# Choosing 80 tokens per expert by counting ranks, with the column copies beside the expert matmuls, in an HGRN scan followed by a capacity-limited expert layer

## The chip, the cores and the metric

One core of a Trainium2 chip runs the whole program. The metric is the time of one execution on the device in microseconds (us), as a median over runs. Times inside the program come from one execution taken by the profiler.

## The reference, cut to what matters

```python
# x, f_logit: (4, 5056, 256); lower_bound: (256,); w_gate: (256, 8)
# w1: (8, 256, 1024); w2: (8, 1024, 256); capacity = 80; all float32
f = lb + (1 - lb) * sigmoid(f_logit)
for t in range(S):                       # S = 5056, per batch and channel
    h = f[:, t] * h + (1 - f[:, t]) * x[:, t];  y[:, t] = h
x = y.reshape(20224, 256)
logits = x @ w_gate;  expert = argmax(logits);  gate = softmax(logits)[expert]
out = zeros((20224, 256))
for e in range(8):
    tok = tokens of expert e, the 80 with the largest gate
    out[tok] = gate[tok] * (relu(x[tok] @ w1[e]) @ w2[e])
```

Every token is scanned, but only 640 of the 20,224 output rows are other than zero.

## The kernel before

The scan works with channels on the 128 partitions. A unit is 512 tokens of one batch: 4 batches times 10 groups give 40 units. `load` fetches the two inputs on SP's queue, `gate` takes the sigmoid on ACT, `enter` multiplies on POOL, `to_channels` transposes both into PSUM on PE (tile tags `sp` and `up`, a bank each, two buffers for `sp` and four for `up`), `decay` writes the decay factors into `h_all` on ACT, and `scan` runs the recurrence in `h_all` on DVE, half of the channels at a time. `logits` (PE) gives the router's logits one unit later, and once for each group of four units `by_token` (an ACT copy `ls` and PE transposes `lt`) and `choice` (four DVE operations) give each token's expert and its distance to the other logits. `h_all` holds all tokens, 158 KB of each partition, and stays until the copies are done.

The kernel is under a manual schedule: each engine carries out its instructions in the order in which the program text emits them. The software pipeline is the loop over `n` at the end of the scan part, in which iteration `n` emits the load of unit `n+3`, `gate` and `enter` of `n+2`, the transposes and `decay` of `n+1`, `scan` of `n`, `logits` of `n-1`, and `by_token` and `choice` when unit `n-2` ends a group. In two places of the loop (after group 4 and after group 9) `gates` finishes five groups in one go: an exponential on ACT, sums and reciprocals on DVE, and for each group two DVE products, a PE transpose and a DVE copy into `cand`.

`cand` has 128 rows, which are 8 experts times 16 (4 batches, and the token's number modulo 4), with 1,264 gate values each; a token's value is in the row of its expert, and the other seven have zero.

Then come, one after the other: `largest(cand)`, which takes the 80 largest of each row with ten rounds of three DVE operations over the row; a trip through DRAM that lays the 16 lists of an expert side by side in `cand2` (8 rows of 1,280); `largest(cand2)`, another ten rounds; eight indirect DMAs that fetch the token numbers; and the copies of 640 columns of `h_all` into `xe`, by DVE, ACT and POOL, each of which first loads 16 token numbers into its registers. Only then is `h_all`'s room given to the weights of experts 1 to 7 (14 of 16 MB), and the experts run: `hidden(e)` scales the columns (DVE), multiplies by `w1` (PE, 32 matmuls) and applies relu (ACT), `result(e)` multiplies by `w2` (PE, 16 matmuls), scales by the gate (DVE) and scatters 80 rows into `out` (POOL). `hidden(e+1)` is emitted before `result(e)`. The zeros of `out` are written by 40 DMAs on SP's queue while the lists are made.

Of the kernel before, what the change touches and what calls it, by code (L numbers as in the profile page):

```python
# [16 lines left out]
P = 128  # L17
TOP = 8
# [4 lines left out]
def kernel(  # L23
# [23 lines left out]
    K = (capacity + TOP - 1) // TOP * TOP  # L47
    assert N % P == 0 and D % P == 0 and F % P == 0 and S % R == 0 and C * E == P
# [14 lines left out]
    def tiles(ap, b, g):  # L63
# [25 lines left out]
    base_row = consts.tile([1, P], F32, name="base_row")  # L89
    nc.gpsimd.iota(base_row, pattern=[[0, E], [S, B], [1, R]], base=0, channel_multiplier=0,  # L90
                   allow_small_or_imprecise_dtypes=True)
    base = consts.tile([P, 1], F32, name="base")
    list_base = consts.tile([E, 1], F32, name="list_base")
    nc.gpsimd.iota(list_base, pattern=[[0, 1]], base=0, channel_multiplier=C * K,
                   allow_small_or_imprecise_dtypes=True)

    cand = consts.tile([P, SEG], F32, name="cand")
    BATCHES = 2
    per_batch = -(-n_grp // BATCHES)
    shift = consts.tile([P, per_batch, C, E], F32, name="shift")  # L100
    nc.gpsimd.memset(shift, 0.0)
    pick = consts.tile([P, n_grp, C], F32, name="pick")

# [4 lines left out]

    with tc.tile_pool(name="ld", bufs=4) as ld, \
# [5 lines left out]
        xs, fs, sts, uts, sps, ups, lgs, lts, gms = ({} for _ in range(9))  # L115
# [6 lines left out]
        def setup():  # L122
            nc.vector.tensor_scalar(omlb, lb, -1.0, 1.0, ALU.mult, ALU.add)
            nc.vector.tensor_scalar(nomlb, lb, 1.0, -1.0, ALU.mult, ALU.add)
            for o in range(DC):
                nc.vector.tensor_scalar_mul(wg[:, o], wg[:, o], omlb[:, ds(o, 1)])
            bp = plg.tile([P, 1], F32, name="bp", tag="lt")
            nc.tensor.transpose(bp, base_row, ident[:1, :1])
            nc.vector.tensor_copy(base, bp)

# [56 lines left out]


        def choice(g):
# [3 lines left out]

            def small(shape, name):
                return gsm.tile([P] + shape, F32, name=name, tag=name)[:n_p]

            mx = small([C], "mx")
            nc.vector.tensor_reduce(mx, lg, AX.X, ALU.max)
            sh = shift[:n_p, g - begin(g)]
            nc.vector.tensor_tensor(sh, lg, mx.unsqueeze(2).broadcast_to(full), ALU.subtract)  # L200
            eq = small([C, E], "eq")
# [6 lines left out]
        def gates(g0, g1):  # L208
            n = g1 - g0
            sh = shift[:, ds(0, n)]  # L210
            nc.scalar.activation(sh, sh, ACT.Exp)
            sm = gsm.tile([P, n, C], F32, name="sm", tag="sm")
            nc.vector.tensor_reduce(sm, sh, AX.X, ALU.add)
            nc.vector.tensor_scalar_add(sm, sm, 1e-9)
            gt = gsm.tile([P, n, C], F32, name="gt", tag="gt")
            nc.vector.reciprocal(gt, sm)
            for g in range(g0, g1):
                n_p = rows(g)
                gm = gsm.tile([P, E, C], F32, name="gm", tag="gm", bufs=2)[:n_p]
                full = [n_p, C, E]  # L220
                oh = gsm.tile([P, C, E], F32, name="oh", tag="oh")[:n_p]
                nc.vector.tensor_tensor(oh, revexp[:n_p].unsqueeze(1).broadcast_to(full),
                                        pick[:n_p, g].unsqueeze(2).broadcast_to(full),
                                        ALU.is_equal)
                nc.vector.tensor_tensor(
                    gm.rearrange("p e c -> p c e"), oh,
                    gt[:n_p, g - g0].unsqueeze(2).broadcast_to(full), ALU.mult)
                gms[g] = gm
                candidates(g)

        def candidates(g):
            n_p = rows(g)
            ct = plg.tile([P, P], F32, name="ct", tag="lt")
            nc.tensor.transpose(ct[:, :n_p], gms.pop(g).rearrange("p e c -> p (e c)"),
                                ident[:n_p, :n_p])
            nc.vector.tensor_copy(cand[:, ds(first(g) // R, n_p)], ct[:, :n_p])
# [9 lines left out]

        ends = sorted({n_grp * i // BATCHES - 1 for i in range(1, BATCHES + 1)} - {-1})
        batches = {g: (ends[i - 1] + 1 if i else 0, g + 1) for i, g in enumerate(ends)}
        AHEAD = 3

        def begin(g):
            return next(g0 for g0, g1 in batches.values() if g0 <= g < g1)

        setup()
        for n in range(-AHEAD, n_unit + 4):
# [10 lines left out]
            group(lambda g: gates(*batches[g]) if g in batches else None, n - 3)  # L266


    EARLY = 1
    w1_sb, w2_sb = [], []  # L270

    def weights(pool, e):
        w1_sb.append(pool.tile([P, DC, F], F32, name=f"w1_sb{e}"))
        nc.sync.dma_start(out=w1_sb[e], in_=w1[e].rearrange("(o p) f -> p o f", p=P))
        w2_sb.append(pool.tile([P, FC, D], F32, name=f"w2_sb{e}"))
        nc.sync.dma_start(out=w2_sb[e], in_=w2[e].rearrange("(c p) d -> p c d", p=P))

    wpool = ctx.enter_context(tc.tile_pool(name="wpool", bufs=1))
    for e in range(EARLY):
        weights(wpool, e)  # L280

    xpool = ctx.enter_context(tc.tile_pool(name="xpool", bufs=1))
    zpool = ctx.enter_context(tc.tile_pool(name="zpool", bufs=1))
    ZR = 4
    zero = zpool.tile([P, ZR * D], F32, name="zero")
    nc.gpsimd.memset(zero, 0.0)
    out_z = out.rearrange("(p k) d -> p (k d)", p=P)
    for k in range(0, N // P, ZR):
        n = min(ZR, N // P - k) * D
        nc.sync.dma_start(out=out_z[:, ds(k * D, n)], in_=zero[:, :n])  # L290

    with tc.tile_pool(name="sel", bufs=1) as sel, \
         tc.tile_pool(name="psl", bufs=1, space=PSUM) as psl, \
         tc.tile_pool(name="psh", bufs=2, space=PSUM) as psh, \
         tc.tile_pool(name="psy", bufs=2, space=PSUM) as psy:


        def largest(src, vals, at):
            for k in range(0, K, TOP):
                top = vals[:, ds(k, TOP)]  # L300
                nc.vector.max(out=top, in_=src)  # L301
                nc.vector.max_index(out=at[:, ds(k, TOP)], in_max=top, in_values=src)  # L302
                if k + TOP < K:
                    nc.vector.match_replace(out=src, in_to_replace=top, in_values=src,  # L304
                                            imm_value=-2.0)

        val = sel.tile([P, K], F32, name="val")
        at = sel.tile([P, K], U32, name="at")
        largest(cand, val, at)
        nc.scalar.dma_start(out=val_dram, in_=val)  # L310
        atf = sel.tile([P, K], F32, name="atf")
        nc.gpsimd.tensor_copy(atf, at)
        ids = sel.tile([P, K], I32, name="ids")
        nc.gpsimd.tensor_scalar(out=ids, in0=atf, scalar1=float(R), scalar2=base,
                                op0=ALU.mult, op1=ALU.add)
        nc.scalar.dma_start(out=id_dram, in_=ids)

        cand2 = sel.tile([E, C * K], F32, name="cand2")
        nc.scalar.dma_start(out=cand2, in_=val_dram.rearrange("(e c) k -> e (c k)", e=E))
        val2 = sel.tile([E, K], F32, name="val2")  # L320
        at2 = sel.tile([E, K], U32, name="at2")
        largest(cand2, val2, at2)
        if capacity < K:
            nc.vector.memset(val2[:, capacity:], -1.0)
        at2f = sel.tile([E, K], F32, name="at2f")
        nc.vector.tensor_copy(at2f, at2)
        nc.vector.tensor_scalar_add(at2f, at2f, list_base)  # L327


        sp = psl.tile([K, 2, E], F32, name="slots")  # L330
        nc.tensor.transpose(sp[:, 0], at2f, ident[:E, :E])  # L331
        nc.tensor.transpose(sp[:, 1], val2, ident[:E, :E])
        place = sel.tile([K, E], I32, name="place")
        nc.vector.tensor_copy(place, sp[:, 0])
        gsl = sel.tile([K, E], F32, name="gsl")
        nc.vector.tensor_copy(gsl, sp[:, 1])
        far = sel.tile([K, E], F32, name="far")
# [3 lines left out]
        id_list = id_dram.rearrange("r k -> (r k)").unsqueeze(1)  # L341
        tok = sel.tile([K, E], I32, name="tok")
        for e in range(E):
            nc.gpsimd.indirect_dma_start(
                out=tok[:, ds(e, 1)], out_offset=None, in_=id_list,
                in_offset=bass.IndirectOffsetOnAxis(ap=place[:, ds(e, 1)], axis=0))
        tokf = sel.tile([K, E], F32, name="tokf")
        nc.vector.tensor_copy(tokf, tok)
        goals = []
        for e in range(E):  # L350
# [96 lines left out]
```

## Time and profile before

| | us |
|---|---|
| median of 3 runs (407.60 to 407.68) | 407.61 |
| the profiled execution | 407.11 |
| its span, first to last instruction | 405.3 |
| DVE busy | 255.1 (63%) |
| PE busy (PE weight loads 153.0) | 200.4 (49%) |
| ACT busy | 134.2 (33%) |
| POOL busy | 129.5 (32%) |

The span is what the timeline's clock counts from; 1.8 us of the profiled execution lie around it. Engines are PE (matmul), PEld (its weight loads), DVE (vector), ACT (scalar), POOL (GpSimd) and SP (which only issues DMAs here); a q behind an engine is its instruction queue. No engine is busy for much more than half of the time, so the busy shares don't say what bounds the kernel: one has to go through its stages in order of time.

### The profile page before, as it was taken

To read this page: it belongs to the slowest core of one execution; us is meant where nothing else is said; L and a number is where in the kernel's file an instruction comes from. 1 tells how busy PE (TensorE), PEld (TensorE's weight loads), DVE (VectorE), ACT (ScalarE), POOL (GpSimd) and SP (SyncE) were. 2 spreads that over 40 slices of the span, in tenths; PEclk is the share of its full clock that TensorE was granted. 3 is DMA by queue.
4 is the path that set the end of the run, shared out by engine and by line. 5 is a ranking of instruction groups with operands and counts; after the bars stand their busy time and mean duration, and the time that the engine had idled before them with its cause. 6 is when DMAs were issued, how large, how long until landed. Compare 5 with 4: busy or idle time off the path is not lost. (4 is left out here: it accounts for less than half of the span.)

```text
span 405.3 us, 5826 instructions
## 1 busy us (share of the span) xinstructions
PE 200.4 (49%) x1718; PEld 153.0 (38%) x1718; DVE 255.1 (63%) x553; ACT 134.2 (33%) x408; POOL 129.5 (32%) x197
## 2 busy tenths in 40 slices
PE   2988999972999996200000000000000039998995
PEld 2866676751766763000000000000000039776773
DVE  0768889886788886699994999942556640001000
ACT  4776767670667763000000000001666501100010
POOL 4868677742477660000000000035670000001001
PEclk9999999996899998555555555555555555999999
DMA  8999999990699926999953000000000029997000
GB/s 245 348 350 349 327 330 281 334 327 20 195 322 320 318 94 204 421 420 420 420 235 134 8 0 1 0 0 0 2 2 1 2 81 377 374 380 266 18 8 16
DMA packets 60015, 80.59 MB, mean 199 GB/s; under 512 B 3400, under 2 KB 52680, under 8 KB 59984
## 3 DMA queue, kind: packets, MB, share of 16 engines
q1 hardware_dynamic: 58496, 79.44, 56.6%
q0 software_dynamic: 640, 0.66, 0.6%
q8 instruction: 13, 0.21, 0.2%
q10 hardware_dynamic: 848, 0.13, 0.2%
q14 instruction: 18, 0.15, 0.1%
HBM read 58.77 MB, written 21.45 MB: 198 GB/s over the span
## 5 line engine op out<-in xcount | busy, mean ns | idle before, releaser
L146 POOL TENSOR_TENSOR x_t<-f_t,x_t 128x1024 f32<-128x1024 f32 x40 | 94.8, 2369 | 53.3 <-ACT f_t L142 41.2
L165 DVE TENSOR_TENSOR_SCAN h_all<-h_all,up 128x512 f32<-128x512 f32 x80 | 95.1, 1253 | 6.9 <-PE up L152 5.7
L375 ACT COPY xe<-h_all 128x2 f32 x256 | 26.2, 190 | 134.2 <-issue 134.2
L159 ACT ACTIVATE h_all<-sp,nomlb 128x512 f32<-128x512 f32 x80 | 50.9, 684 | 44.0 <-PE sp L152 44.0
L394 PE MATMUL h_ps<-xt,w_sb 128*128 128x80 f32 x256 | 36.6, 313 | 55.6 <-DVE xt L386 50.9
L394 PEld LDWEIGHTS h_ps<-xt,w_sb 128*128 128x128 f32 x256 | 35.6, 227 | 58.3 <-DVE xt L386 51.1
L152 PE MATMUL sp<-ident,f_t 128*128 128x128 f32 x320 | 45.9, 290 | 4.2 <-ACT f_t L142 4.2
L152 PE MATMUL up<-ident,x_t 128*128 128x128 f32 x320 | 45.5, 284 | 5.0 <-DVE h_all L165 2.8
L331 PE MATMUL slots<-ident,at2f 8*80 8x8 f32 x1 | 0.2, 200 | 96.4 <-DVE at2f L327 96.4
L177 PE MATMUL lg<-h_all,wg 128*32 128x128 f32 x640 | 44.2, 404 | 6.4 <-ACT ls L182 4.8
L142 ACT ACTIVATE f_t<-f_t 128x1024 f32<-128x1024 f32 x40 | 42.4, 1061 | 9.7 <-DMA f_t<-in_f_logit_dram 9.7
L406 DVE TENSOR_SCALAR y<-y_ps,gsl 80x256 f32<-80x256 f32 x8 | 3.8, 480 | 63.9 <-PE y_ps L403 63.9
L152 PEld LDWEIGHTS sp<-ident,f_t 128*128 128x128 f32 x320 | 37.6, 148 | 16.0 <-ACT f_t L142 10.8
L375 DVE COPY xe<-h_all 128x2 f32 x256 | 30.5, 179 | 19.6 <-issue 19.6
L152 PEld LDWEIGHTS up<-ident,x_t 128*128 128x128 f32 x320 | 38.2, 147 | 7.5 <-DVE h_all L165 3.9
L331 PEld LDWEIGHTS slots<-ident,at2f 8*80 8x80 f32 x1 | 0.1, 135 | 96.7 <-issue 96.7
L407 POOL DMA_INDIRECT out_dram<-y,goal x8 | 7.4, 920 | 90.0 <-DMA w_sb<-in_moe_w_dram 45.6
L301 DVE MAX8 val<-cand 128x8 f32<-128x1264 f32 (+1 forms) x20 | 29.6, 1480 | 5.9 <-DMA cand<-val_dram 5.1
L403 PE MATMUL y_ps<-w_sb,hid 128*80 128x256 f32 x128 | 29.6, 386 | 0.0
L302 DVE FIND_INDEX8 at<-val,cand 128x8 uint32<-128x1264 f32 (+1 forms) x20 | 29.4, 1471 | 0.0
L397 ACT ACTIVATE hid<-h_ps 128x480 f32<-128x480 f32 (+1 forms) x16 | 7.0, 438 | 64.2 <-PE h_ps L394 64.2
L304 DVE MATCH_REPLACE8 cand<-val,cand 128x1264 f32<-128x1264 f32 (+1 forms) x18 | 26.3, 1461 | 0.0
(57 smaller groups left out, 139.8 us busy)
## 6 DMA issues: line engine op xcount, KB each, us to landing
f_t<-in_f_logit_dram SPq DMA_DIRECT2D x40, 512.0 KB, 5.4
x_t<-in_x_dram SPq DMA_DIRECT2D x40, 512.0 KB, 5.7
out_dram<-zero SPq DMA_DIRECT2D x39, 512.0 KB, 10.0
w_sb<-in_moe_w_dram SPq DMA_DIRECT2D x16, 1024.0 KB, 12.8
out_dram<-zero SPq DMA_DIRECT2D x1, 256.0 KB, 2.0
tok<-id_dram,place POOLq DMA_INDIRECT x8, 2.2
out_dram<-y,goal POOLq DMA_INDIRECT x8, 2.3
val_dram<-val ACTq DMA_DIRECT2D x1, 40.0 KB, 1.5
```

The lines of the kernel that those rows point to most:

```text
L142: nc.scalar.activation(sts[n], sts[n], ACT.Sigmoid, scale=-1.0)
L146: nc.gpsimd.tensor_tensor(uts[n], sts[n], uts[n], ALU.mult)
L152: nc.tensor.transpose(ps[:, ds(r * P, P)], src[n][:, r, ds(o * P, P)], ident)
L159: nc.scalar.activation(h_all[:, o, ds(spot(n), G)], sps.pop((n, o)), ACT.Identity, scale=nomlb[:, ds(o, 1)], bias=1.0)
L165: nc.vector.tensor_tensor_scan(h, h, ups.pop((n, o)), h_all[:, o, ds(spot(n) - 1, 1)] if n >= B else 0.0, ALU.mult, ALU.add)
L177: nc.tensor.matmul(lgs[g][ds(r * LC, LC), b], wg[:, o], hv[:, o, :, r], start=o == 0, stop=o == DC - 1, skip_group_check=True)
L301: nc.vector.max(out=top, in_=src)
L302: nc.vector.max_index(out=at[:, ds(k, TOP)], in_max=top, in_values=src)
L304: nc.vector.match_replace(out=src, in_to_replace=top, in_values=src, imm_value=-2.0)
L375: copy(xe[:, :, ds(k + j, 1)], h_all[:, :, ds(v, 1)])
L394: nc.tensor.matmul(h_ps[:, c], w1_sb[e][:, o, ds((c0 + c) * P, P)], xt[:, o], start=o == 0, stop=o == DC - 1, skip_group_check=True)
L403: nc.tensor.matmul(y_ps, hid[:, c], w2_sb[e][:, c], start=c == 0, stop=c == FC - 1)
```

## The change

The branch, the selection, the weights, the copies and the schedule of the gates are new; the scan's own operations are as before. In words:

- The gates are finished in four batches of groups (0 to 3, 4 to 6, 7 and 8, 9), one small job for each loop iteration (`todo`). The product with the reciprocal moves from DVE to POOL. The transposes of a batch share one PSUM bank, `ct`, and `up` has three buffers instead of four.
- `peaks` takes the eight largest of each of 12 parts of every row of `cand` as soon as the part is there (every second column of up to 256). After the loop, the 16 largest of these 96 are the row's candidates.
- A matmul with `mates` gives every row the 256 candidates of its expert, and 16 operations, one for each candidate of a row, count how many are larger. A candidate is taken when the count is under 80. Sums over the rows ahead of it give its slot; 16 matmuls of 80 columns put token numbers and gates into their slots. No list goes through DRAM.
- Four flags for each row say whether 16 candidates might have been too few (`doubts`). They are summed by a matmul beside the experts, and after the experts a branch runs the old lists and the experts again if the sum is over zero.
- Weights come as halves of 512 KB into a ring of seven buffers that has room beside `h_all`: three keys (3 MB) ahead of the selection, the others as the ring's buffers come free.
- Zeros are written by 20 DMAs of 1 MB on ACT's queue, from a source of 2 KB of each partition that is read four times, after the last gates and ahead of the copies.
- Copies of expert `e+2` are emitted ahead of the matmuls of expert `e+1`: 28 columns on DVE, 28 on ACT, 24 on POOL, with one load of as many token numbers each.

```diff
-         tc.tile_pool(name="psu", bufs=4, space=PSUM) as psu, \
+         tc.tile_pool(name="psu", bufs=3, space=PSUM) as psu, \
...
+    def clear(engine, k):
+        n = min(4 * ZW, N // P - k)          # ZW = 2
+        m = n // ZW
+        engine.dma_start(out=out_z[:, ds(k * D, n * D)].rearrange("p (m z) -> p m z", m=m),
+                         in_=zero.unsqueeze(1).broadcast_to([P, m, ZW * D]))
+    clears = range(0, N // P, 4 * ZW)
...
+        def work(g0, g1):
+            jobs = [[lambda: exponentials(g0, g1)], [lambda: sums(g0, g1)]]
+            for g in range(g0, g1 + 1):
+                jobs.append(([lambda g=g: gated(g)] if g < g1 else [])
+                            + ([lambda g=g: turned(g - 1)] if g > g0 else []))
+            jobs.append([lambda: candidates(g0, g1)])
+            mine = [i for i in range(NP) if parts[i][0] == g1 - 1]
+            for i in range(0, len(mine), 2):
+                jobs.append([lambda j=j: peaks(j) for j in mine[i:i + 2]])
+            return jobs
...
+        while n < n_unit + 3 or todo:
...
             group(by_token, n - 2)
             group(choice, n - 2)
-            group(lambda g: gates(*batches[g]) if g in batches else None, n - 3)
+            for job in todo[:1]:
+                for f in job:
+                    f()
+            del todo[:1]
+            group(lambda g: todo.extend(work(*batches[g])) if g in batches else None, n - 2)
+            n += 1
...
+    wring = ctx.enter_context(tc.tile_pool(name="wring", bufs=7))
+    order = [(1, 0)]
+    for e in range(E):
+        order += ([(1, e + 1)] if e + 1 < E else []) + [(2, e)]
...
+    for key in order[:3]:
+        w_sb[key] = weights(*key)            # two DMAs of 512 KB on SP's queue
+    for k in clears:
+        clear(nc.scalar, k)
...
+        nc.vector.max(out=vals[:, :TOP], in_=flat_tops)
+        nc.vector.match_replace(out=rest, in_to_replace=vals[:, :TOP], in_values=flat_tops,
+                                imm_value=-2.0)
+        nc.vector.max(out=vals[:, TOP:], in_=rest)
+        nc.vector.tensor_tensor(spread, ...)                 # 128 x 256
+        nc.tensor.matmul(rivals, mates, spread, ...)
+        for k in range(0, DEEP, TOP):                        # DEEP = 16
+            nc.vector.max_index(out=at[:, ds(k, TOP)], in_max=vals[:, ds(k, TOP)],
+                                in_values=cand)
+        for k in range(DEEP):
+            nc.vector.tensor_scalar(beat, rivals, vals[:, ds(k, 1)], 0.0, ALU.is_gt, ALU.add,
+                                    accum_out=rank[:, ds(k, 1)])
...
+        nc.vector.tensor_scalar(put, at_slot, off[:, 0:1], None, ALU.is_equal)   # 128 x 1280
+        for j in range(DEEP):
+            nc.tensor.matmul(flat_p, what[:, DEEP - 1 - j].rearrange("p i e -> p (i e)"),
+                             put[:, j], start=j == 0, stop=j == DEEP - 1)
+        nc.vector.tensor_copy(trow, flat_p[:E])
...
+    ways = [(mybir.EngineType.DVE, nc.vector.tensor_copy, 28),
+            (mybir.EngineType.Activation, nc.scalar.copy, 28),
+            (mybir.EngineType.Pool, nc.gpsimd.tensor_copy, K - 56)]
...
+            for e in range(2):
+                gather(e)
+                scaled(e)
+            ps = hidden(0)
+            relu(0, ps)
+            more(1)
+            for e in range(E):
+                if e + 2 < E:
+                    gather(e + 2)
+                if e + 1 < E:
+                    ps = hidden(e + 1)
+                    relu(e + 1, ps)
+                    more(1)
+                y_ps = result(e)
+                more(1)
+                if e + 2 < E:
+                    scaled(e + 2)
+                finish(e, y_ps)
+                if e > 0:
+                    scatter(e - 1)
+            scatter(E - 1)
+    experts(False)
+    unsure = nc.values_load(doubt, min_val=0, max_val=4 * P, ...)
+    with tc.If(unsure > 0):
+        ...                                                   # the lists as before
+        experts(True)
```

## Rows read from the trace of the kernel before

**Rows 1.** Timeline: stage borders (start us, us, engine, operation, idle before)

```profile
171.82 1.48 DVE L301 MAX8 val<-cand 128x8 f32<-128x1264 f32 x1 [0.18 <-DMA out_dram<-zero]
...
280.23 0.22 DVE L359 CAST trow<-rp 8x80 int32<-8x80 f32 x1
281.90 1.61 ACT L375 COPY xe<-h_all 128x2 f32 x16 [119.32 <-issue]
285.15 1.89 DVE L375 COPY xe<-h_all 128x2 f32 x16 [1.10 <-issue]
330.70 0.77 DVE L386 TENSOR_SCALAR xt<-xe,omlb 128x80 f32<-128x80 f32 x4
400.73 0.48 DVE L406 TENSOR_SCALAR y<-y_ps,gsl 80x256 f32<-80x256 f32 x1 [2.97 <-PE y_ps L403]
```

**Rows 2.** Timeline of a steady group in the loop, PE and DVE

```profile
60.21 1.04 PE L152 MATMUL up<-ident,x_t 128*128 128x128 f32 x8
...
61.54 9.47 DVE L165 TENSOR_TENSOR_SCAN h_all<-h_all,up 128x512 f32<-128x512 f32 x8
...
64.04 0.66 PE L152 MATMUL up<-ident,x_t 128*128 128x128 f32 x4 [0.30 <-DVE h_all L165]
...
72.80 0.29 DVE L198 TENSOR_REDUCE mx<-lt 128x16 f32<-128x128 f32 x1 [1.78 <-PE lt L185]
...
74.81 9.47 DVE L165 TENSOR_TENSOR_SCAN h_all<-h_all,up 128x512 f32<-128x512 f32 x8
```

**Rows 3.** Timeline: scans around the first gates batch, last scans, and what follows them

```profile
88.07 2.44 DVE L165 TENSOR_TENSOR_SCAN h_all<-h_all,up 128x512 f32<-128x512 f32 x2
...
114.53 9.47 DVE L165 TENSOR_TENSOR_SCAN h_all<-h_all,up 128x512 f32<-128x512 f32 x8
...
153.48 4.79 DVE L165 TENSOR_TENSOR_SCAN h_all<-h_all,up 128x512 f32<-128x512 f32 x4
...
161.85 0.74 ACT L211 ACTIVATE shift<-shift 128x640 f32<-128x640 f32 x1 [0.88 <-DVE eq L202]
```

**Rows 4.** Groups by shape: busy us, mean ns of one, idle before

```profile
L222 DVE TENSOR_TENSOR oh<-revexp,pick 128x128 f32<-128x128 f32 x9 | 2.4, 270 | 0.0
L234 PE MATMUL ct<-ident,gm 128*128 128x128 f32 x9 | 4.2, 469 | 17.3 <-DVE gm L225 17.3
L302 DVE FIND_INDEX8 at<-val,cand 128x8 uint32<-128x1264 f32 x10 | 14.7, 1469 | 0.0
L406 DVE TENSOR_SCALAR y<-y_ps,gsl 80x256 f32<-80x256 f32 x8 | 3.8, 480 | 63.9 <-PE y_ps L403 63.9
```

**Rows 5.** SP's timeline: two of the first eight loads, and all issues of zeros

```profile
0.75 0.43 SPq L134 DMA_DIRECT2D f_t<-in_f_logit_dram  x1
5.39 1.51 SPq L134 DMA_DIRECT2D f_t<-in_f_logit_dram  x1
155.11 66.83 SPq L290 DMA_DIRECT2D out_dram<-zero  x40
```

**Rows 6.** DMA issues: count, KB each, median us from issue to landing

```profile
out_dram<-zero SPq DMA_DIRECT2D x39, 512.0 KB, 10.0
```

**Rows 7.** Stretches: us, busy us of PE, PEld, DVE, ACT, POOL, granted clock, DMA share, GB/s

```profile
20.00:30.00 10.00, 8.81 (x96) 6.32 (x88) 6.70 (x6) 6.88 (x10) 6.96 (x4) 1.00 1.10 350
180.00:190.00 10.00, 0.00 (x0) 0.00 (x0) 9.79 (x11) 0.00 (x0) 0.00 (x0) 0.50 1.03 420
331.00:345.00 14.00, 13.99 (x65) 13.99 (x66) 0.47 (x3) 1.46 (x4) 0.00 (x0) 0.50 0.98 344
349.60:397.30 47.70, 43.41 (x290) 35.65 (x291) 4.54 (x19) 5.25 (x12) 5.54 (x6) 1.00 0.52 183
```

**Rows 8.** Timeline of one expert's turn on PE at the higher clock

```profile
357.96 3.77 PE L394 MATMUL h_ps<-xt,w_sb 128*128 128x80 f32 x32 [0.79 <-issue]
...
361.56 3.62 PE L403 MATMUL y_ps<-w_sb,hid 128*80 128x256 f32 x16
```

**Rows 9.** Register loads of 16 numbers: duration ns min/median/max

```profile
L371 DVEq TENSOR_LOAD <-trow x16: 1097/1100/1345, 280.6 to 327.4; - x16
```

More of the change, by code (lines that the diff above doesn't have):

```diff
@@ new lines @@
+    batches = {g1 - 1: (g0, g1) for g0, g1 in zip([0] + cuts, cuts)}
+    per_batch = max(g1 - g0 for g0, g1 in batches.values())
+    assert per_batch <= 4, "the candidates of a batch share a bank"
+    parts = []
+    for g0, g1 in batches.values():
+        for g in range(g0, g1, 2):
+            lo = first(g) // R
+            hi = first(min(g + 2, g1)) // R if min(g + 2, g1) < n_grp else SEG
+            parts += [(g1 - 1, lo + i, hi) for i in range(2)]
+    NP = len(parts)
+    tops = consts.tile([P, NP, TOP], F32, name="tops")
@@ L186, in by_token, with batch_of, begin @@
             lts[g] = lt.rearrange("p b (r e) -> p (b r) e", e=LC)[:, :, :E]
+        def batch_of(g):
+            return next((g0, g1) for g0, g1 in batches.values() if g0 <= g < g1)
+        def begin(g):
+            return batch_of(g)[0]
         def choice(g):
@@ L279 @@
[L279 to L337, printed above, removed]
@@ new lines, with weights @@
+    wring = ctx.enter_context(tc.tile_pool(name="wring", bufs=7))
+    FH, CH = F // 2, FC // 2
+    order = [(1, 0)]
+    for e in range(E):
+        order += ([(1, e + 1)] if e + 1 < E else []) + [(2, e)]
+    def weights(which, e):
+        halves = []
+        for i in range(2):
+            t = wring.tile([P, DC * FH], F32, name="w_sb", tag="w_sb")
+            if which == 1:
+                t = t.rearrange("p (o f) -> p o f", o=DC)
+                nc.sync.dma_start(out=t, in_=w1[e][:, ds(i * FH, FH)].rearrange(
+                    "(o p) f -> p o f", p=P))
+            else:
+                t = t.rearrange("p (c d) -> p c d", c=CH)
+                nc.sync.dma_start(out=t, in_=w2[e][ds(i * FH, FH)].rearrange(
+                    "(c p) d -> p c d", p=P))
+            halves.append(t)
+        return halves
@@ L342 @@
[L342 to L350, printed above, removed]
-            goal = sel.tile([K, 1], I32, name=f"goal{e}")
-            nc.vector.tensor_tensor(goal, tok[:, ds(e, 1)], far[:, ds(e, 1)], ALU.add)
-            goals.append(goal)
@@ L356 @@
-        rp = psl.tile([E, K], F32, name="rp")
-        nc.tensor.transpose(rp, tokf, ident[:K, :K])
-        trow = xpool.tile([E, K], I32, name="trow")
-        nc.vector.tensor_copy(trow, rp)
-        ways = [(mybir.EngineType.DVE, nc.vector.tensor_copy),
-                (mybir.EngineType.Activation, nc.scalar.copy),
-                (mybir.EngineType.Pool, nc.gpsimd.tensor_copy)]
-        SHARE = 16
-        X = []
-        for e in range(E):
-            xe = xpool.tile([P, DC, K], F32, name=f"xe{e}")
-            for i, k in enumerate(range(0, K, SHARE)):
-                engine, copy = ways[i % len(ways)]
-                n = min(SHARE, K - k)
-                _, at_tok = nc.values_load_multi_w_load_instructions(
-                    trow[ds(e, 1), ds(k, n)], engines=(engine,), min_val=0, max_val=N - 1,
-                    skip_runtime_bounds_check_because="token numbers come from iota")
-                for j, v in enumerate(at_tok):
-                    copy(xe[:, :, ds(k + j, 1)], h_all[:, :, ds(v, 1)])
-            X.append(xe)
```

373 lines of the change are left out of this document (282 added, 91 removed).

## The prediction

> **What bounds the kernel now.** I read the page's busy shares first (no engine is over 63%), then the timeline from border to border. Nothing bounds the whole; six stages follow each other. The scan loop ends with the last scan at 153.48 + 4.79 = 158.3 us [rows 3]. A tail of 13.5 us finishes the gates, until the first MAX8 at 171.8. The lists take 108.4 us, from there to the token numbers at 280.2. Copies take 50.5 us, until the experts' first operation at 330.7. The experts need 70.0 us, to 400.7 where PE ends; 4.6 us remain of the span of 405.3 [rows 1]. In the lists DVE works alone and PE's clock is at its lower level, 1.2 GHz; it stays there for the experts' first 14 us [rows 7].
>
> In the loop, a steady group of four units takes 74.81 - 61.54 = 13.27 us, while its eight scans take 9.47 [rows 2]. PE is the pace: it is busy 8.8 of 10 us [rows 7]. DVE waits 1.78 us for the transposed logits in each group [rows 2].
>
> **1. The loop.** Removed: the gates batch after group 4. From the scans at 88.07 to those at 114.53, each the first of its group, are 26.46 us, 13.19 more than a steady group [rows 3]: -13.2.
>
> Added: a wait on `up`. With four banks PE transposes unit n+1 while DVE still owes unit n. With three, the second transposes of a unit need the bank of the first half of the unit before it, so they wait for that scan. After `choice` this scan is late: it starts at 61.54 and, at 9.47/8 = 1.18 us, ends at 62.72, where PE has needed the bank since 60.21 + 0.52 = 60.7 [rows 2]. PE stands still for 2.0 us, and `logits`, the next unit's transposes and `lt` are queued behind it; for `lt`, DVE waits. Of this 0.3 us comes back, a wait at 64.04 that is then over. I take 1.8 for nine groups: +16. Bounds: 0, if PE finds the time elsewhere in the group, and 2.3 each, if nothing comes back.
>
> Jobs: the transposes of seven groups are now among PE's work, 7 x 0.47 = 3.3 us [rows 4]. The products with the expert masks (0.27 each), sums, copies and peaks cost DVE some 1.6 us per group, which its wait of 1.78 covers as far as a job doesn't stand between `choice` and the next scan; +0.7. Three table switches on ACT get nothing: ACT is busy 6.9 of 10 us [rows 7]. Together +4, bounds 0 and 7. The set-up's dozen DVE operations come before the first data: 0 to 2, I take 0. The last scan ends at 158.3 - 13.2 + 16 + 4 = 165.
>
> **2. The tail.** `choice` is through 3.9 us after the last scan (exponential at 161.85 plus a little) [rows 3]. Behind it come the end of the third batch and the one-group fourth, a chain of about a dozen DVE operations at 0.3, two POOL products and two transposes with their semaphores: 6 us. The selection starts at 165 + 10 = 175; bounds 8.5 and 13.5, today's tail.
>
> **3. The selection** replaces 108.4 us. Three operations over 96 values, 0.7; `spread`, 0.4; two FIND_INDEX8 with their loads, 3.1; 16 rank counts over 256 values in PSUM at 0.48 [rows 4] less the overlap of neighbours, 6.9; flags, PE sums and `off`, 1.4; `put`, 1,280 values, by the FIND_INDEX8 over 1,264, 1.5; 16 matmuls at 14.0/65 = 0.215 on the slow clock [rows 7], 3.4; `trow`, 0.6. Sum 18, bounds 14 and 22. Token numbers at 193. DVE still makes the flags (1.6), loads 28 numbers (1.1 for 16 [rows 9], 1.9 if it goes with the count; I take 1.4) and copies 28 columns at 1.89/16 = 0.118 [rows 1], 3.3: its share is done at 199.3.
>
> **4. The zeros on ACT's queue.** This is what I take to decide the size. Whoever issues DMAs faster than they go is held: SP needed 66.8 us to issue 40 DMAs, and the first loads' issue grew from 0.43 to 1.51 us, the time that 524 KB take at 350 GB/s [rows 5, 7]. Those loads are 512 pieces of 1 KB each, and the fourth was the first that was slow; so some 2,048 pieces are out when the issuer is held. Zeros today (128 pieces each) have eight out: 10.0 us to land at 420 GB/s is 4.2 MB [rows 6, 7]. A new clear has 512 pieces of 2 KB: four out, 4.2 MB.
>
> ACT comes to the clears after the last exponential, at 165 + 4 = 169. Their 20.7 MB go at between 350 (1 KB pieces) and 420 GB/s (4 KB) [rows 7]; I take 385: 53.8 us, and 1.4 for a weight half between them, so to 224. ACT is free 4.2 MB earlier (10.9 us), at 213; with eight out (8.4 MB) at 202. All of ACT's copies are queued behind that, and for them wait `scaled(0)` on DVE, then PE. ACT loads numbers (1.3) and copies 28 at 1.61/16 [rows 1], 2.8: 217. PE starts at 218, 0.7 later; without this, DVE's share would let it start at 200.
>
> The Trainium skill (DMA: Bandwidth & Descriptors, Issuing engines are not separate DMA queues) says that issuing from several engines only saves the sequencer's time, which is usually small beside the transfer. The row of SP's 66.8 us speaks against "small". By the page's sentence ACT would be free by 176 and the total would be that of rival C.
>
> **5. The experts.** From PE's start to its end they take 69.7 us today (331.0 to 400.7 [rows 1, 7]): `hidden` 0 and 1 at the lower clock, 13.8, then turns of 3.77 + 3.62 with a gap of 0.79 [rows 8] in which PE waits for `xt`, which is queued behind `y` on DVE. Six such gaps go, since `scaled` now stands ahead of `finish`: 69.7 - 4.7 = 65.0, turns of 7.2. Copies stay under it: DVE's `finish`, load, copies and `scaled` make 0.5 + 1.4 + 3.3 + 0.5 = 5.7 of 7.2 us, ACT's 4.1 + 0.9, POOL's 24 columns and a scatter 5.6. Weights need 2.1 MB per turn, 6.1 us at 344 GB/s [rows 7]. The last `result` ends at 283. The first scatter, about 235, finds the zeros landed.
>
> **6. The end.** 4.6 us as today [rows 1], and the branch: all engines load a flag after the last scatter, meet, and jump over the second copy of the lists and experts. No row shows a branch; the nearest are the register load (1.1 [rows 9]) and the end itself (4.6). I take 4, bounds 1 and 9. Span 283 + 4.6 + 4 = 292; the execution lies 1.8 above its span (407.1 to 405.3) and the median 0.5 above that: 294.
>
> The Trainium skill (Runtime: NRT & Kernel Launch, Instruction fetch mechanics) says that a jump out of the fetched window waits for its target to be fetched. No run here shows one; with the upper bound of 9 for it the total would be 299.
>
> **The rivals.**
> A. As above, 294 (286 to 304). For it: the scan that ends after PE wants the bank, and the stretched issues [rows 2, 5]. 0.50.
> B. PE finds the `up` wait's time elsewhere: 294 - 16 = 278. For it: PE is not quite full. Against: what is held are all of PE's instructions, in order. 0.14.
> C. The clears don't hold ACT: 294 - 18 = 276; with eight out, 283. Against: the stretched issues [rows 5]. 0.14.
> D. B and C: 260. 0.05.
> E. The copies set the experts' pace: if `hidden` waits for copies queued behind `finish` of the result just before, a turn is 0.5 + 5.2 + 0.5 + 0.3 + 3.6 = 10 us, 2.8 more in seven turns, 294 + 20 = 314. Against: two experts are gathered ahead. 0.14, with slower branch or weights in it.
> F. Slower: the branch is taken. Then the old lists (108.4), zeros, copies for two experts and the experts (70) come behind everything: 294 + 186 = 480. It decides from the first row with a part of eight taken values, or with 16. Worked out from the reference's own inputs, the most that one row gives to its expert's 80 is 12, and the most in one part is 5; equal values at a border are left. 0.03. A change that saves nothing would need this: 90 us of the 108.4 are row searches that are gone.
>
> **How the numbers follow.** About 0.2% is what a measurement of this kernel can tell from no change. Faster is everything but F: 0.96; the same 0.01; slower 0.03. The range 270 to 309 takes in A, B, C and the near end of E, 0.83.
>
> **What would show it.** In the profile after: steady groups of 15 us with PE waiting for the scan at `up` (step 1; 13.3 for B); ACT's queue in clears until about 213 and `scaled(0)` waiting for ACT (step 4; at 176 for C); token numbers 18 us after the first MAX8 over 96 values (step 3); turns of 7.2 us on PE (step 5; 10 for E); 8 to 9 us behind the last `result` (step 6). What would make it wrong above all is the rate of 2 KB pieces and how many may be out.

## The result, and the profile after

The median after the change is 302.92 us (four runs, 301.96 to 304.95) against 407.64 before, a ratio of 0.744 with a 95% interval from 0.740 to 0.748. The forecast was 294, its range 270 to 309: the way and the range were right, the likeliest value was 9 us too low. The profiled execution took 303.26 us, with a span of 301.4. Medians here and below are over all runs of a kernel; one of the four of experiment 2 and two of the four of experiment 7 lie over 1.5% above their fastest, and without these the medians are 286.99 and 266.68.

| stage | before | forecast | after |
|---|---|---|---|
| last scan ends | 158.3 | 165 | 167.7 |
| selection starts | 171.8 | 175 | 177.1 |
| token numbers | 280.2 | 193 | 196.7 |
| ACT free of the clears | no clears there | 213 | 220.2 |
| first expert matmul | 331.0 | 218 | 230.7 |
| last `y` starts | 400.7 | 283 | 295.0 |
| span | 405.3 | 292 | 301.4 |

First the page: busy tenths, granted clock and bytes moved, in 40 slices of 7.5 us.

```profile
PE   1798596979978896979797420610003999999991
PEclk9999899797999998998999955575555559999998
DMA  7999979596979896887920999999994448999900
GB/s 211 349 348 350 341 233 324 198 313 198 290 226 299 249 346 198 242 263 220 318 79 0 335 372 409 409 406 388 384 383 157 142 139 265 312 310 305 327 27 27
```

The long stretch of DVE alone is gone. What is left of a gap on PE lies between slices 23 and 31, and in 23 to 30 the DMA engines are full at 335 to 409 GB/s: the clears. The timeline of that stretch, with one row of each step (start us, us, engine, operation, idle before):

```profile
171.22 49.03 ACTq L147 DMA_DIRECT2D out_dram<-zero  x20
...
177.05 0.26 DVE L419 MAX8 vals<-tops 128x8 f32<-128x96 f32 x1
...
192.26 4.19 PE L472 MATMUL flat_p<-put,what 128*16 128x80 f32 x32 [1.26 <-DVE put L469]
196.48 0.23 DVE L474 CAST trow<-flat_p 8x80 int32<-8x80 f32 x1 [4.37 <-PE flat_p L472]
...
203.13 3.03 POOL L519 COPY xe<-h_all 128x2 f32 x24 [12.56 <-issue]
...
227.46 2.74 ACT L519 COPY xe<-h_all 128x2 f32 x28 [55.96 <-DMA out_dram<-zero]
230.30 0.43 DVE L526 TENSOR_SCALAR xt<-xe,omlb 128x80 f32<-128x80 f32 x2 [21.67 <-ACT xe L519]
230.66 7.09 PE L537 MATMUL h_ps<-xt,w_sb 128*128 128x80 f32 x32 [33.53 <-issue]
```

ACT spends 49.03 us in issuing its 20 clears, until 220.25. `xt` waits 21.67 us for ACT's copies, and PE 33.53 us (put down to "issue" by the profile; its operand is that `xt`). The selection ends at 196.7 and isn't on the path at all: from ACT's first clear to PE's first expert matmul are 59.4 us, whatever DVE does beside.

Between 220.25 and 227.46 ACT does nothing but load 28 numbers into registers. The register loads (duration in ns, least/median/most, first and last start):

```profile
L515 POOLq TENSOR_LOAD <-trow x8: 1537/1573/6077, 196.7 to 271.1; - x8
L515 DVEq TENSOR_LOAD <-trow x8: 1849/1858/7112, 197.7 to 277.6; - x8
L515 ACTq TENSOR_LOAD <-trow x8: 1715/1734/6939, 220.3 to 274.1; - x8
```

The usual one takes 1.5 to 1.9 us; each engine's first takes 6 to 7, and POOL's second and third, which start before 215 us, take 5.8 and 5.9. Before the change 16 numbers took 1.10 [rows 9], with 1.345 as the most.

The loop, one group after the change (compare [rows 2]), PE and DVE:

```profile
65.07 0.29 DVE L268 TENSOR_REDUCE mx<-lt 128x16 f32<-128x128 f32 x1 [3.04 <-PE lt L248]
...
65.74 0.60 PE L215 MATMUL up<-ident,x_t 128*128 128x128 f32 x4
...
67.07 4.78 DVE L228 TENSOR_TENSOR_SCAN h_all<-h_all,up 128x512 f32<-128x512 f32 x4
68.49 0.63 PE L215 MATMUL up<-ident,x_t 128*128 128x128 f32 x4 [2.15 <-DVE h_all L228]
69.05 1.10 PE L240 MATMUL lg<-h_all,wg 128*32 128x128 f32 x16
70.07 1.97 PE L215 MATMUL sp<-ident,f_t 128*128 128x128 f32 x8
71.83 1.70 PE L215 MATMUL up<-ident,x_t 128*128 128x128 f32 x8
...
74.50 1.09 PE L215 MATMUL sp<-ident,f_t 128*128 128x128 f32 x8
```

The second half of `up` waits 2.15 us for the scan behind `choice`, as forecast. Not forecast are the two rows behind it: eight transposes that take 1.09 at 74.50 take 1.97 at 70.07. From 69.8 to 73.2 the granted clock is 0.50, the lower of PE's two levels (1.2 of 2.4 GHz); PE stood still shortly before. The waits of PE in the whole program (us in total, times, longest), then that stretch and two groups (us, PE busy, granted clock, DMA share, GB/s):

```profile
PE up L215 <- DVE h_all L228: 20.3, 11, 3.0
```

```profile
69.80:73.20 3.40, 3.40 (x23) 0.50 0.52 157
```

```profile
65.10:81.60 16.50, 13.83 (x134) 0.90 0.80 241
81.60:97.70 16.10, 12.62 (x134) 1.00 0.86 267
```

The same 134 records take 13.83 us in a group in which the clock fell and 12.62 in one in which it didn't.

The experts (compare [rows 8]) and the end:

```profile
252.96 3.62 PE L552 MATMUL y_ps<-w_sb,hid 128*80 128x256 f32 x16
...
256.42 3.69 PE L537 MATMUL h_ps<-xt,w_sb 128*128 128x80 f32 x32
```

```profile
295.01 0.48 DVE L558 TENSOR_SCALAR y<-y_ps,gsl 80x256 f32<-80x256 f32 x1 [2.97 <-PE y_ps L552]
```

There is no gap in the turns of 7.0 us; from the last `y` to the end of the span are 6.4 us, where 4.6 were before [rows 1].

### The profile page after: what moved, and what is told of

It reads as the page before. It is cut to its first block, busy times and chain, and to the rows that moved or that the text cites. A ratio compares the mean times of both kernels' runs of the same rounds, so it can differ in the third digit from the quotient of the medians.

```text
span 301.4 us, 5943 instructions
## 1 busy us (share of the span) xinstructions
PE 207.6 (69%) x1756; PEld 162.6 (54%) x1756; DVE 180.6 (60%) x484; ACT 133.3 (44%) x380; POOL 135.2 (45%) x269
## 4 chain that ended last, share of the span: by engine, by line
PE 56%; DVE 17%; issue 14%; ACT 5%; DMA 5%; POOL 1%; SPq 0%; POOLq 0%; DVEq 0%; ACTq 0%
PE lg L240 12%; PE h_ps L537 12%; PE y_ps L552 10%; PE sp L215 9%; PE up L215 8%; DVE h_all L228 6%; ACT h_all L222 3%; DVE eq L271 3%; DMA f_t<-in_f_logit_dram 3%; DVE beat L449 3%; PE lt L248 2%; DMA x_t<-in_x_dram 2%; ACT ls L245 2%; PE flat_p L472 1%; DVE mx L268 1%
## 5 line engine op out<-in xcount | busy, mean ns | idle before, releaser
L215 PE MATMUL up<-ident,x_t 128*128 128x128 f32 x320 | 48.3, 293 | 22.2 <-DVE h_all L228 20.3
L519 ACT COPY xe<-h_all 128x2 f32 x224 | 22.2, 190 | 67.3 <-DMA out_dram<-zero 56.0
L215 PE MATMUL sp<-ident,f_t 128*128 128x128 f32 x320 | 48.2, 299 | 3.4 <-ACT f_t L205 3.4
L519 POOL COPY xe<-h_all 128x2 f32 x192 | 24.5, 202 | 39.2 <-DVE xt L526 18.5
L519 DVE COPY xe<-h_all 128x2 f32 x224 | 26.5, 180 | 19.6 <-issue 19.6
L240 PEld LDWEIGHTS lg<-h_all,wg 128*32 128x32 f32 x640 | 18.3, 120 | 19.2 <-ACT ls L245 7.0
L552 PEld LDWEIGHTS y_ps<-w_sb,hid 128*80 128x80 f32 x128 | 19.4, 156 | 8.1 <-issue 1.0
L561 POOL DMA_INDIRECT out_dram<-y,goal x8 | 7.5, 940 | 34.9 <-DVE y L558 32.5
L268 DVE TENSOR_REDUCE mx<-lt 128x16 f32<-128x128 f32 (+1 forms) x10 | 2.9, 291 | 28.0 <-PE lt L248 28.0
L526 DVE TENSOR_SCALAR xt<-xe,omlb 128x80 f32<-128x80 f32 x16 | 3.5, 258 | 23.6 <-ACT xe L519 22.8
L545 ACT ACTIVATE hid<-h_ps 128x320 f32<-128x320 f32 x16 | 7.0, 436 | 20.8 <-PE h_ps L537 20.8
```

Source lines behind the costliest of these rows:

```text
L215: nc.tensor.transpose(ps[:, ds(r * P, P)], src[n][:, r, ds(o * P, P)], ident)
L240: nc.tensor.matmul(lgs[g][ds(r * LC, LC), b], wg[:, o], hv[:, o, :, r], start=o == 0, stop=o == DC - 1, skip_group_check=True)
L519: copy(X[e][:, :, ds(k + j, 1)], h_all[:, :, ds(v, 1)])
L552: nc.tensor.matmul(y_ps, hid[:, c], halves[c // CH][:, c % CH], start=c == 0, stop=c == FC - 1)
L561: nc.gpsimd.indirect_dma_start(out=out, out_offset=bass.IndirectOffsetOnAxis(ap=goal[:, ds(e, 1)], axis=0), in_=Y.pop(e), in_offset=None, ...
```

## The experiments

All are edits of the changed kernel; a ratio, where there is one, is to the kernel before. Spans and stage times come from one profiled execution each.

**1. Without the clears.** Are clears the whole of PE's late start, and of the long register loads?

```diff
-    for k in clears:
-        clear(nc.scalar, k)
```

> The 20 DMAs that write zeros are left out, so the rows of the output that no expert writes are not set. Theory (the zeros hold ACT and, while they run, also slow the register loads): the token numbers come at 196.7 us as before, register loads of 28 numbers take the 1.7 to 1.9 us that they take late in the changed kernel, ACT's first copy is at about 198.5 instead of 227.5, DVE's copies of the first expert end at about 203 and PE starts the experts at about 204 instead of 230.7; total about 276 us. Rival 1 (the first register loads are slow for another reason, such as fetching instructions): they still take 6 to 7 us without zeros, PE starts at about 209, total about 281. Rival 2 (the experts wait for something else, such as weights): PE starts after 215, total above 287.

Measured: 279.05 us (one run), span 277.2. Timeline around the token numbers, and ACT's loads:

```profile
198.91 0.23 DVE L472 CAST trow<-flat_p 8x80 int32<-8x80 f32 x1 [4.61 <-PE flat_p L470]
...
201.32 2.74 ACT L517 COPY xe<-h_all 128x2 f32 x28 [27.50 <-issue]
...
206.59 1.75 PE L535 MATMUL h_ps<-xt,w_sb 128*128 128x80 f32 x7 [7.05 <-issue]
```

```profile
L513 ACTq TENSOR_LOAD <-trow x8: 1727/1737/1924, 199.2 to 250.1; - x8
```

PE starts 7.7 us after the token numbers' row instead of 34.2, and the first load takes 1.92 instead of 6.94. So both the hold and the long loads come with the clears. The 3 us by which the time is above the expectation lie at the start of the loop (last section).

**2. The clears on SP's queue,** which has nothing to do then but weights. Is it ACT that counts, or the transfers?

```diff
-        clear(nc.scalar, k)
+        clear(nc.sync, k)
```

> Only the queue of the zeros changes, ACT's to SP's, behind the first 3 MB of weights. Theory (ACT's hold and the slow register loads under the zeros are two costs): ACT is free at 171, its first load starts at 196.7 but takes 6 to 7 us since the zeros still run until about 229; DVE's copies end at about 208.6 and PE starts at about 209.5. The second and third expert's loads are slow too, and the fourth key of the weights is queued behind the zeros until about 230, so part of the 21 us is given back: PE's third hidden stage starts at about 235 instead of 249.4, total about 289 us. If the slow loads were ACT's own matter: total about 282. Rival (the zeros hold the experts whoever issues them, by the register loads or the weights): PE's third hidden stage not before 245, total 299 or more.

Measured: 287.52 us (285.67 to 291.59), ratio 0.704 (0.702 to 0.707).

```profile
203.58 2.74 ACT L519 COPY xe<-h_all 128x2 f32 x28 [32.54 <-issue]
...
208.72 7.09 PE L537 MATMUL h_ps<-xt,w_sb 128*128 128x80 f32 x32 [12.02 <-issue]
...
219.36 7.12 PE L537 MATMUL h_ps<-xt,w_sb 128*128 128x80 f32 x32 [3.44 <-DVE xt L526]
```

It was ACT: PE starts 22 us earlier with the same bytes in flight. SP is the one that is held now, for 51.0 us (167.4 to 218.4), and PE waits for no weights. But only 15.4 us arrive at the end. The register loads that lie beside the clears stay at 6 to 7 us on all three engines, and there are more of them now, so `hidden(1)` waits for `xt`; the experts take 69 us instead of 64. ACT's loads:

```profile
L515 ACTq TENSOR_LOAD <-trow x8: 1737/2480/7037, 196.3 to 256.6; - x8
```

**3 and 4. Two ways to take away the wait for the third bank.** One moves `choice` behind the scan of the next unit, so that no scan is late. The other gives `up` its fourth bank back: each group's transposed gates go into the bank of `lt` and are copied out group by group.

```diff
             unit(scan, n)
+            group(choice, n - 3)
             unit(logits, n - 1)
             group(by_token, n - 2)
-            group(choice, n - 2)
```

> The choice of a group is emitted one iteration later, behind the next unit's scan, so that DVE doesn't wait for the logits ahead of that scan; three banks for the second transposes stay. Theory (PE waits for the scan that stands behind the choice, and its clock falls in that wait): the wait of 2 to 3 us in each group is gone, groups take 13.3 to 13.7 us instead of 16.1 to 17.0, the last scan ends at about 142 instead of 167.7 and everything behind it moves by as much; total about 278 us. Rival (the long groups come from the jobs that are now spread over the loop): groups stay at 16 or more, total about 303.

```diff
-         tc.tile_pool(name="psu", bufs=3, space=PSUM) as psu, \
+         tc.tile_pool(name="psu", bufs=4, space=PSUM) as psu, \
...
-                cts[g0] = plg.tile([P, per_batch, P], F32, name="ct", tag="ct")
+            ct = plg.tile([P, P], F32, name="ct", tag="lt")
...
+            nc.vector.tensor_copy(cand[:, ds(first(g) // R, n_p)], ct[:, :n_p])
```

> The bank is given back: four for the second transposes; the transposed gates go through the bank of the logits again, a group at a time, each copied at once. Everything else as in the changed kernel. Theory (the third bank is what makes PE wait): PE's wait for the scan after the choice falls from 2 to 3 us to the 0.3 of the kernel before, groups without such a transpose take 13.3 us, those with one up to 1 us more, the last scan ends at about 145 and the total is about 281 us. Rival (the spread jobs make the groups long): groups stay at 16 or more, total about 303.

Measured: late choice 282.02 us (281.63 to 282.77), ratio 0.691 (0.689 to 0.692); four banks 285.48 (one run). The stretch of 65.1 to 81.6 us of late choice, then of four banks, as above, and the first and last `mx` (start us) of the kernel before, the changed kernel, four banks and late choice:

```profile
65.10:81.60 16.50, 14.98 (x162) 1.00 1.05 336
```

```profile
65.10:81.60 16.50, 14.66 (x156) 1.00 0.99 311
```

```profile
L198 DVE TENSOR_REDUCE mx<-lt x10: 291/291/292, 32.1 to 160.9; 128x16 f32<-128x128 f32 x9, 112x16 f32<-112x128 f32 x1
```

```profile
L268 DVE TENSOR_REDUCE mx<-lt x10: 290/291/293, 32.3 to 169.9; 128x16 f32<-128x128 f32 x9, 112x16 f32<-112x128 f32 x1
```

```profile
L268 DVE TENSOR_REDUCE mx<-lt x10: 291/292/292, 32.5 to 153.4; 128x16 f32<-128x128 f32 x9, 112x16 f32<-112x128 f32 x1
```

```profile
L268 DVE TENSOR_REDUCE mx<-lt x10: 257/292/292, 35.7 to 149.0; 128x16 f32<-128x128 f32 x9, 112x16 f32<-112x128 f32 x1
```

In both the clock stays at 2.4 GHz in this stretch and the DMA engines are full. From the first `mx` to the last are 128.8 us before the change, 137.6 after, 120.9 with four banks, 113.3 with the late choice. So the third bank costs 137.6 - 120.9 = 16.7 us (the fourth bank has ten small copies instead of four, which is in it). The late choice gains 7.6 more: DVE no longer stands waiting for `lt` in each group, which it does for 1.77 us with four banks, just as before [rows 2]. A steady group of four banks takes 13.27 us like that of before, one of late choice 12.7. Groups with jobs are longer: 14.2 to 14.8 us with four banks, and with late choice 16.2 and 16.1 in two, in which a batch's exponential runs. Both kernels end some 4 us above what was expected (278 and 281); these groups are one part of it. Of the 7.6 us only 3.5 show between the two times: the loop of late choice began 2.5 us later in the profiles (last section), and its clears held ACT for 49.6 us instead of 47.2.

The clears start when the loop ends: at 150.3 us instead of 171.2 with the late choice, and PE's first expert matmul is at 210.2, 59.9 us behind. The token numbers are there at 175.0, 35 us ahead of that matmul: the selection isn't on the path here either.

**5. Pieces of 1 KB** instead of 2 KB, in the same 20 DMAs. What holds the issuer?

```diff
-    ZW = 2
+    ZW = 1
...
-        n = min(4 * ZW, N // P - k)
+        n = min(8 * ZW, N // P - k)
...
-    clears = range(0, N // P, 4 * ZW)
+    clears = range(0, N // P, 8 * ZW)
```

> The changed kernel with the clears written in pieces of 1 KB instead of 2 KB (same 20 DMAs of 1 MB, twice the pieces). Theory: what holds ACT is the number of pieces that its queue takes (some 4,096 out), so two DMAs are out instead of four when ACT is held: ACT free some 5 us nearer to the last clear's landing, near 226 us. Rival: it is bytes or DMAs that count: four DMAs out as before, ACT free some 8 to 10 us before the last landing. On the register loads: if they wait behind outstanding pieces, the first of each engine goes from 6 to 7 us to about twice that; if behind the writes as such, it stays at 6 to 7.

(The 4,096 in it is a slip: four DMAs of 512 pieces are 2,048.) Measured: 312.11 us (one run), span 310.2.

```profile
172.29 57.45 ACTq L147 DMA_DIRECT2D out_dram<-zero  x20
236.54 2.75 ACT L519 COPY xe<-h_all 128x2 f32 x28 [63.96 <-DMA out_dram<-zero]
```

Neither side's time came out, because the rate fell to 338 to 349 GB/s. ACT is free at 229.7, and the bytes stop near 236.2, 6.5 us later; with 2 KB pieces it was 220.2 and some 229.1, 8.9 us. At the rate of each that is 2.2 and 3.4 MB out, or some 2,200 and 1,700 pieces. At the start, two clears were issued freely (0.4 and 0.6 us) before one took 5.2 us, with 2 KB three before one took 4.3. The hold is not a fixed number of bytes or of DMAs; pieces are nearer, but they don't agree either. The register loads are as long as before (ACT 6.5, DVE 7.2 us), so they don't go by the number of pieces.

**6. Without the branch** and the path under it, which rows would take for which 16 candidates don't do.

```diff
-    unsure = nc.values_load(doubt, ...)
-    with tc.If(unsure > 0):
-        ...
-        experts(True)
```

> The changed kernel without the branch at its end and the code under it (this leaves out the path for rows whose 16 largest do not do). Theory: from the last result's end to the end of the span 4.6 us as before the change, instead of 6.4, so the branch costs 1.8 us: span about 299.6. Rival 1: the 6.4 us are the last scatter's landing, and nothing changes. Rival 2: the branch costs 4 us, as the prediction had it, of which something is hidden: below 3 us at the end.

Measured: 302.25 us (one run), span 300.4.

```profile
295.88 0.48 DVE L558 TENSOR_SCALAR y<-y_ps,gsl 80x256 f32<-80x256 f32 x1 [2.98 <-PE y_ps L552]
```

300.4 - 295.9 = 4.5 us of end instead of 6.4: a branch that isn't taken costs some 1.9 us here (one run; the ends of all profiles with the branch are 6.2 to 6.8 us). (This loop, too, began 3 us late, see the last section, so the whole time says little.)

**7. Late choice and clears on SP** (edits 2 and 3 together). Do the gains add?

> The changed kernel with both edits that gained by themselves: the choice of a group one unit later (alone 282.0 us against 302.9) and the clearing of the result on SP's queue (alone 287.5). Theory: the two gains lie in different stages (loop and gap ahead of the experts) and add: 302.9 - 20.9 - 15.4 = 266.6 us; by stages, token numbers at 174.8, then 12.6 to the first expert matmul as with the clears on SP, experts 68.8, end 6.3, so a span of 262.5 and some 265 us. Rival: with the experts earlier the writes lie over more of their turns, so register loads of 6 to 7 us in ACT and POOL set the pace of two turns more, and 275 to 280 us come out.

Measured: 268.83 us (265.58 to 270.01), ratio 0.659 (0.657 to 0.662). They add, to 2 us. In the profile the experts take 71.1 us instead of 68.8, so the rival had a part in it: `hidden(1)` waits 3.2 us for `xt`, as in experiment 2, and `hidden(2)` waits 2.2 us for weights, which stand behind the clears in SP's queue:

```profile
211.40 0.87 PE L537 MATMUL h_ps<-xt,w_sb 128*128 128x80 f32 x6 [2.22 <-DMA w_sb<-in_moe_w_dram]
```

**8 to 10. Clears ahead of the weights.** As 7, with 14, 16 or all 20 clears issued right behind the last input load, when the transfers would stand idle.

```diff
             unit(load, n + AHEAD)
+            if n + AHEAD == n_unit - 1:
+                for k in clears[:14]:
+                    clear(nc.sync, k)
...
-    for k in clears:
+    for k in clears[14:]:
         clear(nc.sync, k)
```

> As the run before it, but 14 of the 20 clears are issued on SP right behind the last input load, ahead of the experts' first weights, and 6 behind those. Theory: the transfers, idle from about 133 to 147 us, take the writes then, the last clear lands near 193 instead of 205, so fewer of the experts' turns lie beside writes: experts 65 to 66 instead of 68.8, 260 to 262 us. The first register loads at 175 us still lie beside writes or weights; if they are as short as without clears (1.9 instead of 7) 256. Rival: the first weights come behind 14 MB of clears and PE waits for them at 187, or the last input loads are slowed: 266 or more.

> As the run with 14 clears ahead of the first weights, with 16 there and 4 behind. There the register loads at 171.8 us lay beside weights and took 1.8 and 1.9 us, those at 176.5 and 185 beside the last 6 clears and took 5.7 to 7.3. Theory (a register load is long only while clears are under way): the early clears end near 171, the first loads stay short, the first expert matmul stays near 179, and the later clears end near 190 instead of 195, so one long load fewer lies in the turns: 1 to 3 us less, 253 to 255. Rival (the weights, not the loads, set the start of the experts): they come 5 us later and so does the first matmul, 184, and 258 or more.

> As the run before it with all 20 clears ahead of the first weights. Theory: clears are under way until some 183 us, so the first register loads (at 172) take 6 to 7 us instead of 1.9 and the first expert matmul is at 184 instead of 179; behind that no load lies beside a clear and the experts take 64.3 us instead of 68.3: about the same sum, 255 to 258. Rival (loads are slowed by any traffic): the first loads and all others beside the weights are as long, and experts over 68: 260 or more. Rival (weights set the start): the first matmul only near 187.

Measured: 14 early clears 256.05 us (253.62 to 257.40), ratio 0.627 (0.622 to 0.631); 16: 257.05, 0.629 (0.628 to 0.630); 20: 264.56, 0.646 (0.644 to 0.649). The first loads with 14, SP's issues of that kernel, and PE's start with 20:

```profile
L518 ACTq TENSOR_LOAD <-trow x1: 1920/1920/1920, 171.8 to 171.8; - x1
```

```profile
159.48 7.18 SPq L389 DMA_DIRECT2D w_sb<-in_moe_w_dram  x4
166.71 3.86 SPq L393 DMA_DIRECT2D w_sb<-in_moe_w_dram  x2
170.61 14.74 SPq L147 DMA_DIRECT2D out_dram<-zero  x6
```

```profile
193.55 7.09 PE L540 MATMUL h_ps<-xt,w_sb 128*128 128x80 f32 x32 [19.15 <-DMA w_sb<-in_moe_w_dram]
```

With 14, the loads at 171.8 us lie beside 3 MB of weights at some 370 to 395 GB/s and take 1.8 to 2.1 us; PE starts 7 us behind the token numbers. The loads at 176.5, beside the last six clears, take 5.7 to 6.6. So it isn't traffic as such that makes them long but the clears. With 16, the first loads still meet clears (4.7 to 5.4 us): PE starts 9.9 us behind the token numbers instead of 7.3, and the experts take 64.9 us instead of 68.4. So gain and loss nearly balance, and the two times can't be told apart (0.622 to 0.631 and 0.628 to 0.630). PE's start at 184 is that of the rival, but what PE waits for there is `xt` (9.26 us), not weights. With 20 the rival decides: PE waits 19.15 us for weights that stand behind the clears. The best version, with 14, is 47 us faster than the changed kernel.

## Why the prediction was right, and what it mis-sized

**Step 1, the loop: right in sum, by the right wait.** Forecast -13.2 + 16 + 4 = +6.8; from first to last `mx` it came to 137.6 - 128.8 = +8.8. Of these the bank is 16.7 against 16, and all the rest -7.9 against -9.2. But the working behind the 16 missed the clock. PE's five groups at 0.89 or 0.90 have 0.4 to 1.4 us more busy time each than the 12.62 of the group at 1.00, 5.2 together, and PE's waits for the scan are 20.3 us, against 2.6 with four banks. That is some 23 us more for PE, of which only 16.7 are seen at the end: some 6 came back elsewhere in the groups, where the forecast gave back 0.3 of each 2.0. These are two misses of opposite sign, and that the 16 came so near is in part luck. "PE is the pace" was half of it: the late choice shows that 0.6 us of each 13.27 were DVE's wait for `lt`.

**Step 2** was right: the selection starts 9.3 us behind the last scan, forecast 10.

**Step 3** took 19.7 us to the end of `trow`, forecast 18: the 16 counts came at 0.53 instead of 0.43 (8.4 for 6.9), the matmuls on the slow clock took 4.2 for 3.4, `put` 0.9 for 1.5. That the matmuls came near is luck: the trace has two records for each matmul of the program (the 32 matmuls given for `hidden` and the 16 for `result` are records too), so there are 32 of 0.13 us here, where the forecast had 16 of 0.215. The forecast put it off the path, and there it is.

**Step 4, the clears: right in kind, and here the 9 us were lost.** ACT is held, as the stretched issues [rows 5] had it, and rival C (no hold, 276) is out: ACT issued for 49.0 us. The Trainium skill (DMA: Bandwidth & Descriptors, Issuing engines are not separate DMA queues) calls the sequencer's time that other engines save usually small. The trace disagrees here: moving the same DMAs to an idle queue gave 15.4 us. The terms of PE's start, 230.7 for 218: clears began at 171.2 instead of 169 (+2.2); the hold was 49.0 instead of 44 (+5.0); and ACT's register load was 6.9 instead of 1.3 (+5.6). In the hold the rate came out, 387 GB/s from 171.2 to 229.7 us for 385. But these are 22.6 MB, of which 20.7 are clears: 1.9 MB of weights lay between, where the forecast had one half of 0.5 MB, and that is some 3 us. The other 2 are the 3.4 instead of 4.2 MB that are out when ACT comes free. The register load is the term that failed in kind: [rows 9] show loads at a time when no clears were under way, and the forecast took their price as if it held beside them. Experiment 1 shows that it doesn't.

**Step 5**: 64.3 us for 65.0, turns of 7.0 for 7.2. The copies stay under the turns, and E (314) is out.

**Step 6**: 6.4 us for 8.6; the branch costs 1.9 and not 4. Of the jump that waits for its target (the Trainium skill, Runtime: NRT & Kernel Launch, Instruction fetch mechanics) there can be no more than these 1.9 us in this case.

The sum of the errors along the path: 12.7 us at PE's start, -0.7 in the experts, -2.2 at the end, 9.8 in the span (301.4 for 291.6). **Rival B** (the bank's wait is absorbed, 278) is out: the wait is there, and without it the time is 285.48 (four banks). **F** (the branch taken) didn't happen: 6.4 us at the end leave no room for it.

## What to carry to other kernels

An engine that issues many large DMAs can be held by them, here for 49.0 us: before a queue is chosen, ask what that engine has to do next, and whether another queue is idle. A transfer that nobody needs early, like clearing, belongs where the transfers idle, behind the last input but not ahead of data that is waited for (256 us with 14 of the 20 clears there, 265 with all). When a buffer is taken away from a pipeline, look for the one consumer that comes late in each round; reordering that consumer can be worth more than the buffer (282.0 us against 285.5).

## What the runs showed of the hardware that was not expected

**Register loads beside clears.** Loads of 24 to 28 numbers take 1.5 to 1.9 us without clears (each engine's first 1.8 to 2.1), and no more than these beside weights at some 370 to 395 GB/s, but 4.7 to 7.3 us beside the clears, on ACT, DVE and POOL alike, with pieces of 1 or 2 KB, and with the clears on ACT's or SP's queue. Whether it is the writes to DRAM or the reads of the zeros' source that they wait for was not tried.

**The clock falls after a short stand.** After 2.15 us of waiting at 66.3 to 68.5, transposes ran at 1.2 GHz from 69.8 to 73.2; after the wait of 2.15 that ended at 85.06 they didn't (the group at 1.00 above). Of the six such waits of 2.1 to 3.0 us in the loop, the clock fell in or behind five; it fell behind none of the four of 0.8 to 1.7. What tells the sixth apart stays open.

**Three microseconds at the start.** In some profiled executions the first `mx` is at 32.1 to 32.5 us, in others at 34.9 to 35.8 (seven of the twelve profiles, none of the two with four banks). DVE's small set-up operations are long when they start beside a product of POOL (late choice):

```profile
10.19 2.36 POOL L209 TENSOR_TENSOR x_t<-f_t,x_t 128x1024 f32<-128x1024 f32 x1 [0.51 <-DMA x_t<-in_x_dram]
10.26 2.31 DVE L186 TENSOR_SCALAR place<-col_f,row_f 128x16 f32<-128x16 f32 x1
...
13.33 2.31 DVE L191 TENSOR_SCALAR mates<-col_f,row_f 128x128 f32<-128x128 f32 x1
...
17.15 0.69 PE L215 MATMUL up<-ident,x_t 128*128 128x128 f32 x2 [2.89 <-DVE h_all L228]
```

`place` took 0.23 us in the profiled execution of the changed kernel and 2.31 here, where it began 0.07 us behind the product and ended 0.02 behind it. Three operations were hit here, two in the changed kernel's own profile, and the first scan is 2.8 us later (15.88 for 13.08); with three banks PE then waits for it, 2.89 us against 0.42, and its next eight transposes still take 1.91 us, against 1.04 in the changed kernel's profile. The count goes with the start in all profiles: three long set-up operations in each of the seven late ones, two in the four early ones that have these operations. Four banks' profile is one of these four, so it doesn't show what a late start would do there. Step 1 had set 0 to 2 us for the set-up. That POOL's product is what DVE waits for is read from these times alone; the Trainium skill (Trainium Architecture — The Big Picture, What this means for kernel authors) says that the two engines share a port and lock each other out, and these rows agree.
